# Longer score bursts from step 32, wider feed-forward groups and a re-ranked instruction order in a fused attention and feed-forward kernel

## The chip, the core and the metric

The kernel runs on one core of one Trainium2 chip. That core has a matrix engine (TensorE, PE in the profile; its weight loads are the row PEld), a vector engine (VectorE, DVE), a scalar engine (ScalarE, ACT), a general engine (GpSimd, POOL), an engine that issues transfers (SyncE, SP), and 16 DMA engines. Matmuls write to PSUM, all other tiles lie in SBUF.

The metric is the device time of one execution in microseconds. The kernel before took 552.31 us in the median of 3 runs (551.3 to 552.72). The profiled execution took 550.8 us, and its span from the first to the last instruction was 549.0 us.

## The reference

Thresholded attention over 64 heads (8 batches of 8) of 576 rows and width 64, and after it a gated feed-forward layer over the 4608 rows that result:

```python
scores = q @ k.T / 8
scores = where(scores >= max(scores) - tau, scores, -1e9)     # per row, tau 0.02
attn   = exp(scores - max(scores)) / (sum + 1e-9)
x      = (attn @ v), heads side by side                       # 4608 x 512
xn     = x / sqrt(mean(x * x) + 1e-6) * rms_g
out    = (silu(xn @ w_gate) * (xn @ w_val)) @ w_out           # 512 -> 1536 -> 512
```

Inputs and the output are float32. Scores are computed from float32 operands; the products with `v` and all of the feed-forward layer use float16 operands.

## The kernel before

A **step** is 128 rows of scores for one pair of heads; there are 144 of them. Four steps make a **chunk**: 128 complete rows of `x`. There are 36 chunks. One step goes through these stages:

- S: TensorE writes the scores of both heads into PSUM (`s_ps[0]`, `s_ps[1]`, two banks of 512 columns each, one buffer).
- TTR: VectorE copies them to SBUF with the sign turned and keeps the row's extreme value.
- GpSimd makes the threshold; ScalarE and GpSimd make the masked exponentials (`wsb`).
- `wsb` is transposed, by TensorE with a VectorE copy in the first 16 steps and by a DMA afterwards (`wt`).
- AV: after every second step, TensorE multiplies by `v`; VectorE divides by the row sums (`half`).
- After a whole chunk: square, mean, norm, and a DMA that transposes it to `xnT`.

The feed-forward layer takes **groups** of 2 or 4 chunks. For each of the 12 slices `fc` of 128 hidden columns, four gate matmuls and four value matmuls fill one PSUM buffer each (`ring`, four buffers, and the four banks of `s_ps` when the last scores have been read); ScalarE makes a tanh, VectorE makes the silu and the gated product `hf`. Output matmuls follow, with an evacuation `osb` and a store.

Each such piece of work is an `Op` with an engine, a guessed cost, a priority and its dependencies. A list scheduler fixes the order of each engine's instructions when the program is built; nothing is reordered on the chip by it.

```python
                k = (t + (BIAS if other else 0.0), o.prio, i)   # earliest start first, then priority
                if cand is None or k < cand:
                    cand = k
```

Scores go in bursts. One step has its own burst up to step `SB`; from there a burst fills 1024 columns, which is 1.78 steps:

```python
    def plan_bursts():
        plan = [([(s, 0, S, ROW_AT)], s, [[(s, 0, S // 2, ROW_AT), (s, S // 2, S, 512)]])
                for s in range(min(SB, len(steps)))]
        end = S * (len(steps) - SB)
        for at in range(0, end, 1024):
            ...                                  # segments of one or more steps, split at the bank
            plan.append((segs, SB + at / S, [r for r in runs if r]))
```

```python
    # S: every burst waits for the TTRs of the burst before
    deps = [x for d, _, _ in info.values() for x in d] + last_ttr
    ...
    nc.tensor.matmul(s_ps[h][rows, at:at + hi - lo], lhs(hs), kT[i][p][h][hs, lo:hi], start=True, stop=True)   # L581
    ...
    # TTR: one per head and segment, a step that is cut between two bursts has two per head
    nc.vector.tensor_tensor_reduce(                                                                           # L614
        out=ssb_of(s)[:, h, lo:hi], in0=s_ps[h][:, at:at + hi - lo], in1=zrow[:, lo:hi], scale=-1.0 / 8.0, ...
        accum_out=(mx if last else mxp)[m][:, h:h + 1])
    t = ttr_of[s, h] = add("DVE", ..., s - 1 + TTR_PRIO, made + [o_c] + held + before, ttr)
```

```python
    # feed-forward, n = 128 * chunks of the group
            def gmm(o, fs=fs):
                for d in range(4):
                    nc.tensor.matmul(ring[o.slot[0]][:, 0:n], wg[d][:, fs], xnT[slot][:, d, 0:n], ...)        # L854, vmm is L859
            def tanh(...):  nc.scalar.activation(out=th[i][:, 0:n], ...)                                      # L868
            def silu(...):  nc.vector.scalar_tensor_tensor(out=sl[i][:, 0:n], ...)                            # L871
            def gate(...):  nc.vector.tensor_tensor(out=hf[hi][:, 0:n], ...)                                  # L876
    # output: L924 (L899 in the last group), its evacuation on ScalarE (L939) or VectorE (L937)
            on_dve = streamed and not late or not streamed and OUT_DVE[ci % len(OUT_DVE)]
```

Other lines of the profile: L306 transposes q and k on TensorE and L319 (VectorE) and L317 (ScalarE) copy them to `qkt`; L715 and L724 transpose `wsb` on TensorE and copy it in the first 16 steps; L748 and L753 are AV; L770 and L771 are `half`; L788 to L800 are the norm of a chunk.

Of the kernel before, what the change touches and what calls it, by code (L numbers as in the profile page):

```python
# [13 lines left out]
LAT = dict(PE=200.0, ACT=130.0, DVE=175.0, POOL=20.0, SP=0.0)  # L14
SELF = dict(PE=0.0, ACT=125.0, DVE=178.0, POOL=0.0, SP=0.0)
COST = dict(
    s_main=965.0, s_virt=960.0, tr_qk=530.0, tr4=230.0, tr_full=440.0, av_main=290.0, av_virt=370.0, ffn4=215.0, warm=3500.0,
    evac_qk=600.0, evac_qk_act=465.0, evac_half=252.0, evac_kt=330.0, evac_kt_act=252.0, prelu=667.0, exp2=1060.0, exp1=666.0, exp0=590.0,
    mask_d=680.0, mask_g=1810.0, take_g=1360.0, trw=510.0, evac_w=400.0, evac_wp=900.0, rz=210.0, xmul=341.0, sq=612.0, xn=773.0,
    pool_tiny=302.0, pool_mean=944.0, pool_dma=880.0, cast_v=620.0, cast_vt=475.0, cast_w=665.0,  # L20
# [1 line left out]
)  # L22
DMA_NS = dict(qk=1250.0, tl=700.0, v=880.0, vt=350.0, wt=1700.0, xt=800.0, out=800.0, w=820.0, wo=2500.0)
SWITCH = 125.0


class Op:
# [16 lines left out]
def order_ops(ops, ring_sizes):  # L44


    import heapq

    ring_free = {r: [(0.0, i) for i in range(n)] for r, n in ring_sizes.items()}
    users = {}  # L50
    left = {}
    for i, o in enumerate(ops):
        left[i] = len(o.deps)
        for d in o.deps:
            users.setdefault(id(d), []).append(i)
    pending = {}
    for i, o in enumerate(ops):
        pending.setdefault(o.eng, [])
        if not left[i]:
            pending[o.eng].append(i)  # L60
    eng_free = {e: 700.0 for e in pending}
    dma_free = 0.0
    mode = 0
    out = []
    ready_at = {i: 0.0 for i in range(len(ops))}
    while len(out) < len(ops):
        best = None
        for e, lst in pending.items():
            if not lst:
                continue  # L70
            t0 = eng_free[e]
            cand = None
            for i in lst:
                o = ops[i]
                t = max(t0, ready_at[i])
                if o.ring is not None:
                    free = [f for f in ring_free[o.ring] if o.pick is None or f[1] in o.pick]
                    if len(free) < o.nring:
                        continue
                    t = max(t, sorted(free)[o.nring - 1][0])  # L80
                other = e == "PE" and o.mode != mode
                t = max(t, o.release)
                if o.bulk:
                    t = max(t, dma_free - BACKLOG)
                k = (t + (BIAS if other else 0.0), o.prio, i)
                if cand is None or k < cand:
                    cand = k
            if cand is not None and (best is None or cand < best[0]):
                best = (cand, e)
        (t, _, i), e = best  # L90
        o = ops[i]
        cost = o.cost
        if e == "PE":
            if o.mode != mode:
                t -= BIAS
                cost += SWITCH
            mode = o.mode
        o.start = t
        if o.ring is not None:
            o.slot = []  # L100
            for _ in range(o.nring):
                got = min(f for f in ring_free[o.ring] if o.pick is None or f[1] in o.pick)
                ring_free[o.ring].remove(got)
                o.slot.append(got[1])
        eng_free[e] = t + cost
        if o.dma:
            dma_free = max(dma_free, t + 300.0) + o.dma
            o.end = max(dma_free, t + o.cost) + (LAT_TR if o.cost == COST["sp_tr"] else LAT_LD if o.bulk else 2000.0)
        else:
            o.end = t + cost  # L110
        if o.frees is not None:
            ring_free["R"].append((o.end + LAT[o.eng], o.frees[0].slot[o.frees[1]]))
        for slot in o.opens:
            ring_free["R"].append((o.end + LAT[o.eng], slot))
        pending[e].remove(i)
        out.append(o)
        for j in users.get(id(o), []):
            u = ops[j]
            wait = 60.0 if o.dma else SELF[o.eng] if u.eng == o.eng else LAT[o.eng]
            ready_at[j] = max(ready_at[j], o.end + wait)  # L120
            left[j] -= 1
            if not left[j]:
                pending[u.eng].append(j)
    return out
# [3 lines left out]
def kernel(  # L128
# [12 lines left out]
    nc = tc.nc  # L141
    B, H, S, D = q.shape
    NT, DM = out.shape
# [61 lines left out]
    hf = [sb(f"hf{i}", [128, 512], FP16) for i in range(12)]  # L205
    hf += [stg.bitcast(FP16)[:, 512 * i:512 * (i + 1)] for i in range(NHF - 12)]
    osb = [sb(f"osb{i}", [128, DM]) for i in range(2)]

    s_ps = [ps(f"s_ps{h}", 1024) for h in range(2)]
    ROW_AT = 512 - S // 2  # L210
# [356 lines left out]
    def emit_burst(segs, prio, runs):  # L567
# [5 lines left out]
        for run in runs:  # L573
            def fn(o, run=run):
                for s, lo, hi, at in run:
                    _, whole, quads = info[s]
                    p = steps[s][1]
                    for rows, i, lhs in quads if no_whole or o.quad else whole:
                        for h in range(2):
                            hs = HALF[h]  # L580
                            nc.tensor.matmul(s_ps[h][rows, at:at + hi - lo], lhs(hs), kT[i][p][h][hs, lo:hi],  # L581
                                             start=True, stop=True)

            n = sum(hi - lo for _, lo, hi, _ in run)
            o = add("PE", COST["s_main"] * n / S if not no_whole else COST["s_virt"] * n / S, prio if not made else -600.0,
                    deps + made[-1:], fn, mode=2 if no_whole else 1)
            if not made and REL_N[0] <= prio < REL_N[1]:
                o.release = REL[0] + REL[1] * prio
            made.append(o)
# [13 lines left out]
        for s, lo, hi, at in segs:  # L603
# [7 lines left out]
            for h in range(2):  # L611
                def ttr(o, s=s, lo=lo, hi=hi, at=at, h=h, first=first, last=last):
                    m = s % 6
                    nc.vector.tensor_tensor_reduce(  # L614
                        out=ssb_of(s)[:, h, lo:hi], in0=s_ps[h][:, at:at + hi - lo], in1=zrow[:, lo:hi],
                        scale=-1.0 / 8.0, scalar=3.0e38 if first else mxp[m][:, h:h + 1], op0=ALU.add, op1=ALU.min,
                        accum_out=(mx if last else mxp)[m][:, h:h + 1])

                before = [] if first else [ttr_of[s, h]]
                t = ttr_of[s, h] = add("DVE", 75.0 + (hi - lo) / 0.96, s - 1 + TTR_PRIO, made + [o_c] + held + before, ttr)  # L620
                last_ttr.append(t)

    last_ttr = []
# [1 line left out]
    ssb_user = {}  # L625

    def plan_bursts():
        plan = [([(s, 0, S, ROW_AT)], s, [[(s, 0, S // 2, ROW_AT), (s, S // 2, S, 512)]]) for s in range(min(SB, len(steps)))]
        end = S * (len(steps) - SB)
        for at in range(0, end, 1024):  # L630
            segs, runs = [], [[], []]
            stop = min(end, at + 1024)
            x = at
            while x < stop:
                s, lo = divmod(x, S)
                n = min(S - lo, stop - x)
                segs.append((SB + s, lo, lo + n, x - at))
                x += n
            for s, lo, hi, col in segs:
                for bank in range(2):  # L640
                    a, b = max(col, 512 * bank), min(col + hi - lo, 512 * bank + 512)
                    if a < b:
                        runs[bank].append((s, lo + a - col, lo + b - col, a))
            plan.append((segs, SB + at / S, [r for r in runs if r]))
        return plan

    def emit_softmax(s):
# [183 lines left out]
    def emit_ffn(slot, parts, ready_step, pace, streamed):  # L831
# [6 lines left out]
        clock[0] = st + pace * n / 512.0  # L838
        xops = [t for _, t in parts]
        hs = []  # L840
        mm = 4 * (COST["ffn4"] if n == 512 else 112.0 if n == 256 else 60.0)
        el = n / 0.96 + 65.0
        uses = []
        for fc in range(NFC):
# [42 lines left out]
        if streamed:  # L887

            acc = None

            turns = [(fc, tuple(range(len(parts)))) for fc in range(NFC - BY_ROW)]
            turns += [(fc, (j,)) for j in range(len(parts)) for fc in range(NFC - BY_ROW, NFC)]
            last_out = {}
            for n_, (fc, js) in enumerate(turns):
                hi, m_ = hs[fc]

                def omm(o, fc=fc, hi=hi, js=js, first=acc):
                    for j in js:
                        nc.tensor.matmul(ring[(first or o).slot[j]], hf[hi][:, 128 * j:128 * (j + 1)], wo[:, fc],  # L899
                                         start=(fc == 0), stop=(fc == NFC - 1))  # L900

                late = len(js) == 1 and js[0]
# [9 lines left out]
        for j, (ci, _) in enumerate(parts):  # L912
            kind, b, c = chunks[ci]
            pr = st + dt * (NFC + (j + OUT_AT) * (NFC / len(parts) if SPREAD and not streamed else 1.0))
            oi = count["o"] % 2
            count["o"] += 1
            if streamed:
                mo, at = acc, j
            else:
                mo, at = None, 0  # L920
                for lo in range(0, NFC, OUT_PART):
# [124 lines left out]
            o.fn(o)  # L1046


PACE = 13.0
SQ_DVE = (0,)  # L1050
OUT_DVE = (0,)
LAGS = ()
SB = 64
TTR_PRIO = 1.0
BY_ROW = 4
ACC = (4, 6)
OPENS = ((4,), (6,))
NHF = 24
SPREAD = True
OUT_AT = 0.0  # L1060
PART_PRIO = 1.0
SIZES = (2, 2, 2, 2, 4, 4, 4, 4, 4, 4, 2, 2)
LAG = 16.0
LAT_TR = 3000.0
LAT_LD = 2000.0
REL = (0.0, 0.0)
# [64 lines left out]
```

## Time and profile before

| engine | busy us | share of the span |
|---|---|---|
| PE | 540.8 | 98% |
| VectorE | 434.0 | 79% |
| ScalarE | 450.8 | 82% |
| GpSimd | 323.3 | 59% |

How to read the profile that follows in the prediction:

- "Busy" of TensorE counts each matmul from its start to its modelled end, and matmuls overlap. What a group of matmuls takes from the engine's time is read in the timeline, as the distance from its start to the start of the next group.
- A timeline line holds the start in us, the duration in us of the merged lines, the engine, the source line, the operation, what it writes and reads, the shape, and how many instructions it merges. A piece in square brackets is idle time before it and what ended it.
- The chain of waits starts at the last instruction and goes back to what released each one.
- In the list of waits the columns are who waited, for whom, the total in us, how often, and the longest one.

The same stages in five stretches of the execution, as busy us of each engine:

| stretch, us | PE | VectorE | ScalarE | GpSimd |
|---|---|---|---|---|
| 10 to 30 | 18.54 | 16.15 | 18.96 | 8.11 |
| 30 to 60 | 28.55 | 26.65 | 26.59 | 24.29 |
| 60 to 210 | 149.88 | 122.80 | 134.51 | 102.83 |
| 210 to 477 | 266.66 | 225.31 | 238.85 | 180.50 |
| 477 to 549 | 68.35 | 39.07 | 28.24 | 6.65 |

The last scores are computed at 477 us; after that only AV of the last steps and the feed-forward layer remain. Step 64, where the longer bursts begin, lies at about 218 us.

### The profile page before, as it was taken

What the parts mean: (1) busy time and instruction counts of PE and PEld (TensorE: products, weight loads), DVE (VectorE), ACT (ScalarE), POOL (GpSimd) and SP (SyncE); (2) the same over time, 40 slices, a digit from 0 to 9 for tenths busy, and PEclk for the clock granted to TensorE, in tenths of its full rate; (3) what the DMA queues carried; (4) which work ended last, traced back from release to release, by engine and by line L of the source; (5) the groups of instructions that cost most, each with busy time, mean ns of one, the idle gap of its engine ahead of it and who ended that gap; (6) DMA issues with size and microseconds to landing.
All of it is one profiled execution on the core that took longest, in us unless ns stands there. A gap on an engine that the chain in (4) does not pass through costs nothing.

```text
span 549.0 us, 15126 instructions
## 1 busy us (share of the span) xinstructions
PE 540.8 (98%) x5664; PEld 313.9 (57%) x5664; DVE 434.0 (79%) x1251; ACT 450.8 (82%) x741; POOL 323.3 (59%) x462
## 2 busy tenths in 40 slices
PE   8999999999999999999999999999999999999997
PEld 4656766666667555545555556555655454455764
DVE  4898978888778688878896889798897889775633
ACT  5999888999888889788988899899899988853332
POOL 2377955876777567665767466677767665631000
PEclk9999999999999999999999999999999999999999
DMA  9999999869998698798998698999897666740111
GB/s 197 263 297 267 160 186 212 160 127 190 179 200 175 133 169 156 165 196 158 177 204 154 129 193 184 187 168 213 179 178 158 125 124 90 157 95 29 40 59 57
DMA packets 270025, 89.07 MB, mean 162 GB/s; under 512 B 252544, under 2 KB 262272, under 8 KB 269952
## 3 DMA queue, kind: packets, MB, share of 16 engines
q1 hardware_dynamic: 267168, 86.02, 78.8%
q0 software_dynamic: 1600, 1.57, 1.9%
q8 instruction: 44, 0.72, 0.5%
q10 hardware_dynamic: 1184, 0.52, 0.3%
q14 instruction: 29, 0.24, 0.2%
HBM read 37.75 MB, written 9.44 MB: 86 GB/s over the span
## 4 chain that ended last, share of the span: by engine, by line
PE 92%; DVE 3%; ACT 2%; DMA 1%; POOL 1%; issue 1%; SPq 0%; DVEq 0%
PE s_ps L581 28%; PE ring L854 16%; PE ring L859 16%; PE ring L924 15%; PE ring L753 6%; PE ring L306 2%; PE ring L748 2%; DVE ssb L614 2%; PE s_ps L859 1%; PE s_ps L854 1%; DMA stg<-in_moe_w_gate_dram 1%; PE s_ps L899 1%; PE s_ps L924 1%; ACT ssb L663 1%; PE s_ps L264 1%
## 5 line engine op out<-in xcount | busy, mean ns | idle before, releaser
L614 DVE CUSTOM_DVE_ANT_0 ssb<-s_ps,zrow 128x576 f32<-128x576 f32 (+8 forms) x288 | 182.1, 669 | 25.8 <-PE s_ps L581 21.6
L663 ACT ACTIVATE ssb<-ssb,nth 128x576 f32<-128x576 f32 x224 | 166.5, 767 | 21.7 <-POOL nth L652 21.3
L581 PE MATMUL s_ps<-qkt 64*64 64x288 f32 (+16 forms) x1688 | 158.2, 415 | 2.2 <-DVE mx L614 1.8
L696 POOL TENSOR_SCALAR wsb<-ssb,nth 128x576 f16<-128x576 f32 x64 | 110.6, 1729 | 8.9 <-DMA wt<-wsb 2.7
L581 PEld LDWEIGHTS s_ps<-qkt 64*64 64x64 f32 (+1 forms) x1688 | 77.1, 144 | 59.2 <-issue 20.0
L854 PE MATMUL ring<-xnT,wg 128*128 128x256 f16 (+1 forms) x536 | 109.7, 327 | 0.1
L859 PE MATMUL ring<-xnT,wv 128*128 128x256 f16 (+1 forms) x536 | 109.7, 327 | 0.0
L652 POOL TENSOR_SCALAR nth<-mx 128x2 f32<-128x2 f32 x144 | 31.9, 222 | 107.5 <-DVE mx L614 94.5
L670 ACT ACTIVATE wsb<-ssb 128x1152 f16<-128x1152 f32 x80 | 92.8, 1160 | 1.5 <-DMA wt<-wsb 0.4
L871 DVE SCALAR_TENSOR_TENSOR sl<-th,ring 128x512 f32<-128x512 f32 (+1 forms) x134 | 73.6, 551 | 24.4 <-ACT th L868 23.7
L701 POOL TENSOR_TENSOR wsb<-wsb,esb 128x576 f16<-128x576 f16 x64 | 82.0, 1281 | 9.4 <-ACT esb L682 4.9
L868 ACT ACTIVATE th<-ring 128x512 f32<-128x512 f32 (+1 forms) x134 | 64.4, 482 | 21.5 <-PE ring L854 18.2
L859 PEld LDWEIGHTS <-wv 128*128 128x128 f16 x576 | 52.9, 98 | 41.9 <-issue 8.7
L854 PEld LDWEIGHTS <-wg 128*128 128x128 f16 x576 | 53.2, 98 | 39.9 <-issue 6.6
L614 DVE CUSTOM_DVE_ANT_0 ssb<-s_ps,zrow,mxp 128x128 f32<-128x128 f32 (+7 forms) x80 | 38.2, 515 | 24.4 <-PE s_ps L581 24.0
L682 ACT ACTIVATE esb<-ssb,nth 128x576 f16<-128x576 f32 x64 | 49.2, 769 | 7.2 <-POOL nth L652 7.0
L753 PE MATMUL ring<-va,wt 128*128 128x65 f16 (+1 forms) x1280 | 50.9, 193 | 0.0
L924 PE MATMUL ring<-wo,hf 128*128 128x512 f16 x204 | 48.4, 379 | 0.0
L753 PEld LDWEIGHTS <-wt 128*128 128x128 f16 (+1 forms) x1280 | 46.1, 100 | 3.0
L667 ACT ACTIVATE wsb<-ssb 128x576 f16<-128x576 f32 x64 | 43.6, 681 | 1.1
L924 PE MATMUL ring<-wo,stg 128*128 128x512 f16 x180 | 42.2, 379 | 0.0
L876 DVE TENSOR_TENSOR hf<-ring,sl 128x512 f16<-128x512 f32 (+1 forms) x68 | 38.3, 563 | 4.0
(71 smaller groups left out, 566.7 us busy)
## 6 DMA issues: line engine op xcount, KB each, us to landing
vst<-in_v_dram SPq DMA_DIRECT2D x32, 256.0 KB, 3.6
qkn<-in_k_dram SPq DMA_DIRECT2D x31, 256.0 KB, 4.5
out_dram<-osb SPq DMA_DIRECT2D x31, 256.0 KB, 2.7
qkn<-in_q_dram SPq DMA_DIRECT2D x28, 256.0 KB, 4.5
stg<-in_moe_w_gate_dram SPq DMA_DIRECT2D x6, 512.0 KB, 6.3
stg<-in_moe_w_val_dram SPq DMA_DIRECT2D x6, 512.0 KB, 6.1
wt<-wsb SPq DMA_TRANSPOSE x128, 3.4
wo<-in_moe_w_out_dram POOLq DMA_DIRECT2D x4, 384.0 KB, 6.7
```

The lines of the kernel that those rows point to most:

```text
L581: nc.tensor.matmul(s_ps[h][rows, at:at + hi - lo], lhs(hs), kT[i][p][h][hs, lo:hi], start=True, stop=True)
L614: nc.vector.tensor_tensor_reduce(out=ssb_of(s)[:, h, lo:hi], in0=s_ps[h][:, at:at + hi - lo], in1=zrow[:, lo:hi], scale=-1.0 / 8.0, scalar ...
L663: nc.scalar.activation(out=sb_[:, h], in_=sb_[:, h], func=PRELU, scale=-1.0, bias=nth[m][:, h:h + 1], **PRELU_KW)
L670: nc.scalar.activation(out=wsb[s % NW], in_=sb_, func=AF.Exp)
L696: nc.gpsimd.tensor_scalar(out=wsb[s % NW][:, h], in0=sb_[:, h], scalar1=nth[m][:, h:h + 1], scalar2=None, op0=ALU.is_le)
L701: nc.gpsimd.tensor_tensor(out=wsb[s % NW][:, h], in0=wsb[s % NW][:, h], in1=esb[es], op=ALU.mult)
L753: nc.tensor.matmul(ring[o.slot[0]][rs, at:at + D + 1], w[:, 5 * h + j, rs], va[vi][:, p, 2 * j + h], start=False, stop=(h == 1 and j == 3))
L854: nc.tensor.matmul(ring[o.slot[0]][:, 0:n], wg[d][:, fs], xnT[slot][:, d, 0:n], start=(d == 0), stop=(d == 3))
L859: nc.tensor.matmul(ring[o.slot[0]][:, 0:n], wv[d][:, fs], xnT[slot][:, d, 0:n], start=(d == 0), stop=(d == 3))
L868: nc.scalar.activation(out=th[i][:, 0:n], in_=ring[g.slot[0]][:, 0:n], func=AF.Tanh, scale=0.5)
L871: nc.vector.scalar_tensor_tensor(out=sl[i][:, 0:n], in0=th[i][:, 0:n], scalar=1.0, in1=ring[g.slot[0]][:, 0:n], op0=ALU.add, op1=ALU.mult)
L924: nc.tensor.matmul(ring[(first or o).slot[0]], hf[hs[fc][0]][:, 128 * j:128 * (j + 1)], wo[:, fc], start=(fc == 0), stop=(fc == NFC - 1))
```

## The change

Five things change; the arithmetic stays what it was.

1. Bursts of 1024 columns begin at step 32 and no longer at step 64.
2. The feed-forward groups are 2, 2 and eight times 4 chunks; before they were 2, 2, 2, 2, six times 4, 2, 2. The last group, whose output matmuls are interleaved with its gate and value matmuls, so has 4 chunks and uses all four banks of `s_ps` as accumulators. Its third and fourth result use free score buffers as staging.
3. The evacuations of the output go to VectorE and no longer to ScalarE (`OUT_DVE`).
4. Feed-forward work is paced at 16 steps per 4 chunks (before 13) and released 8 steps after its chunks (before 16).
5. The scheduler adds a fixed offset to the priority of each kind of work (`RANK`), and its guesses of some costs are changed. That moves instructions on every engine's queue. `HOLD` is empty, so the first key of the order is the earliest start, as before.

It is for fewer switches between kinds of matmul on TensorE, for fewer half-width matmuls, and for an order in which TensorE waits less.

```diff
-    s_main=965.0, s_virt=960.0, tr_qk=530.0, tr4=230.0, tr_full=440.0, av_main=290.0, av_virt=370.0, ffn4=215.0, warm=3500.0,
+    s_main=965.0, s_virt=960.0, tr_qk=570.0, tr4=230.0, tr_full=440.0, av_main=300.0, av_virt=370.0, ffn4=215.8, warm=3500.0,
...
+RANK = dict(
+    ACT={"emit_ffn/ev": 110, "emit_ffn/store": -50, "emit_ffn/tanh": -20, ... "emit_qk/ev": -40, "emit_softmax/ex": 10, "emit_softmax/prelu": 60, ...},
+    DVE={"emit_av/half": -120, "emit_burst/ttr": 31, "emit_ffn/ev": 250, "emit_ffn/gate": 90, "emit_ffn/silu": 29, ... "emit_qk/ev": 90, "emit_softmax/ev": 180, ...},
+    PE={"emit_av/fn": 1, "emit_burst/fn": -1.1, "emit_ffn/gmm": 5.1, "emit_ffn/omm": 4.4, "emit_ffn/vmm": 0.7, ...},
+    POOL={...}, SP={...},
+)
...
+    for o in ops:
+        if o.prio > -90.0:
+            path = o.fn.__qualname__.split(".")
+            o.prio += RANK[o.eng].get(..., 0.0)
...
-                k = (t + (BIAS if other else 0.0), o.prio, i)
-                if cand is None or k < cand:
-                    cand = k
+                t += BIAS if other else 0.0
+                opts.append((t, o.prio, i))
+            if opts:
+                soon = min(opts)[0] + HOLD.get(e, 0.0)
+                cand = min((x for x in opts if x[0] <= soon), key=lambda x: (x[1], x[0], x[2]))
...
+    osb += [ssb[0][:, 0, 0:DM], ssb[0][:, 0, 0:DM], ssb[1][:, 0, 0:DM], ssb[2][:, 0, 0:DM]]
...
     def plan_bursts():
-        plan = [... for s in range(min(SB, len(steps)))]
-        end = S * (len(steps) - SB)
-        for at in range(0, end, 1024):
+        plan, s = [], 0
+        for lo, hi in CHOP:
+            plan += [... for x in range(s, lo)]
+            end = S * (hi - lo)
+            for at in range(0, end, 1024):
...
-PACE = 13.0
+PACE = 16.0
+HOLD = {}
-OUT_DVE = (0,)
+OUT_DVE = (1,)
-SB = 64
-TTR_PRIO = 1.0
+CHOP = ((32, 144),)
+TTR_PRIO = 0.0
-ACC = (4, 6)
-OPENS = ((4,), (6,))
+ACC = (4, 5, 6, 7)
+OPENS = ((4, 5), (6, 7))
-PART_PRIO = 1.0
-SIZES = (2, 2, 2, 2, 4, 4, 4, 4, 4, 4, 2, 2)
-LAG = 16.0
+PART_PRIO = 2.0
+SIZES = (2, 2, 4, 4, 4, 4, 4, 4, 4, 4)
+LAG = 8.0
```

## The prediction

> **What bounds the kernel now.** I read the page's first two parts first, then the chain, then the timeline of TensorE in three places, and last the list of waits.

> ```profile
> PE 540.8 (98%) x5664; PEld 313.9 (57%) x5664; DVE 434.0 (79%) x1251; ACT 450.8 (82%) x741; POOL 323.3 (59%) x462
> ...
> PE   8999999999999999999999999999999999999997
> ...
> PE 92%; DVE 3%; ACT 2%; DMA 1%; POOL 1%; issue 1%; SPq 0%; DVEq 0%
> ```

> The reader should see that TensorE is on the path nearly from end to end: 98% busy, and 92% of the chain that ended last. A busy share says little by itself when matmuls overlap, so I read starts in the timeline. Two places, steps with a burst of their own and bursts of 1024 columns:

> ```profile
> 154.78 0.60 PE L854 MATMUL ring<-xnT,wg 128*128 128x256 f16 x4
> 155.22 0.60 PE L859 MATMUL ring<-xnT,wv 128*128 128x256 f16 x4
> 155.66 0.60 PE L854 MATMUL ring<-xnT,wg 128*128 128x256 f16 x4
> 156.19 1.20 PE L581 MATMUL s_ps<-qkt 64*64 64x288 f32 x16
> 157.32 0.61 PE L859 MATMUL ring<-xnT,wv 128*128 128x256 f16 x4
> ```
> ```profile
> 223.21 1.03 PE L859 MATMUL ring<-xnT,wv 128*128 128x512 f16 x4
> 224.17 1.96 PE L581 MATMUL s_ps<-qkt 64*64 64x128 f32 x32
> 226.06 1.04 PE L854 MATMUL ring<-xnT,wg 128*128 128x512 f16 x4
> 226.93 1.03 PE L859 MATMUL ring<-xnT,wv 128*128 128x512 f16 x4
> ```

> From start to start: four matmuls of 256 columns take 0.44 us, of 512 columns 0.87. A single step's scores take 1.13 and the group ahead of them 0.53 in place of 0.44, so entering a score burst costs another 0.09. A burst of 1024 columns takes 1.89, and the 512-column group ahead of it 0.96 in place of 0.87. The same four numbers recur wherever I look between 65 and 545 us, so nearly all of this time is work of TensorE, not waiting. Waiting stands at the start:

> ```profile
> PEld s_ps L581 <- DVE mx L614: 6.5, 14, 0.9
> ...
> PE s_ps L581 <- DVE mx L614: 1.8, 5, 0.4
> ```

> These lines are the list of waits for 0 to 65 us alone: TensorE waits for VectorE to empty `s_ps`. The chain from 36 to 52 us shows how:

> ```profile
> 47.73 0.66 DVE ssb L614
> 48.39 0.01 DVE mx L614
> 48.40 0.60 DVE qkt L319
> 49.00 0.66 DVE ssb L614
> 49.66 0.02 DVE mx L614
> 49.69 0.04 issue
> 49.73 1.20 PE s_ps L581 x14
> ```

> A copy of `qkt` stands between the two TTRs of one step, and the next scores (49.73) wait for the second TTR. I estimate the waiting of TensorE at some 14 us up to 65 us: 14 steps from the scores at 12.10 to those at 55.28 in the chain are 3.08 us each, while the work in a step (1.13 scores, about 0.5 transposes, 0.3 AV, some qkt transposes) is about 2.2; that is 12, and about 2 in the fill before.

> [...] the group at 226.06 is busy for 1.04 us, but the next begins after 0.87. [...] 0.87 / 4 is 217 ns, 0.44 / 4 is 110. [...] the copy holds the TTR behind it for 0.60 us. [...]

> **The change part by part.** Counts are from the two instruction orders that the programs were built with.

> (a) Bursts. Steps 32 to 63 lose 32 single bursts, 24 in four quarters (64*64) at 1.13 and 8 in two halves (64*128) at 1.08 (207.19 to 208.27 in the timeline): 27.1 + 8.6 = 35.7 us, with entry 32 x 0.09 = 2.9, together 38.6. They gain 18 long bursts, 12 at 1.89 and 6 with half-form parts at 1.83 to 1.89, say 1.85: 22.7 + 11.1 = 33.8, and 18 x 0.09 = 1.6, together 35.4. Difference: -3.2 us, all on TensorE's path.

> (b) Groups. 144 gate and value groups of 256 columns become 48, and 144 of 512 become 192. 96 x 0.44 = 42.2 go, 48 x 0.87 = 41.8 come: -0.4 us. Output matmuls, AV and transposes keep their counts.

> (c) Order in the first 16 steps. In the order before, four steps up to the first silu have a copy or a `half` between their two TTRs; in the order after none has, and one `qkt` copy less stands before the first silu. The copies move to where VectorE waits for scores anyway (0.67 us before the TTR at 42.06). Four times 0.6 is 2.4; some of it returns as another wait, so -2 us.

> (d) Single steps between 143 and 161 us are delayed in the kernel before: the scores at 152.38 take 1.79 in place of 1.13. These are long bursts afterwards: I take -1 us, half of what I see there.

> (e) VectorE gains 32 evacuations at 0.69 us (L937) = 22 us, and TTRs of 32 more steps in cut form. TTR is busy 62.75 us for 44 single steps between 65 and 210, 1.43 each, and 126.11 us for 80 steps after that, 1.58: +5. It loses 48 of the 72 narrow silu and gate pairs (0.84) and gains 24 wide ones (1.37): -7. So 434 + 20 = 454, 83% of the span. ScalarE loses 33 evacuations (0.585) and 4 us of tanh: 451 - 23 = 428. Both stay beside TensorE; no change of the time.

> (f) Tighter spots. From the last AV of a group to its first gate matmul the order leaves 8.2, 9.0 and 9.1 us of TensorE work in three of ten groups (by the slots above); before, the least was 8.8 and all others were over 11. The path in between is seen at the end of the kernel before: AV ends at 493.8, the transposing DMA is issued at 496.91 and lands 2.8 us later, about 6 us with no queue in the way. Two or three us are left for queues on VectorE, ScalarE and SyncE. I charge +1 us in all.

> Sum: -3.2 - 0.4 - 2 - 1 + 1 = -5.6. The gap between span and device time stays. 552.3 - 5.6 = 546.7; with the new order tuned as a whole, I lean a little lower: **546.0 us**.

> **The rivals.** *VectorE becomes the bound.* Between 210 and 477 us it is busy 225.3 of 267 us, 84%; with one evacuation of 0.69 per 14 us it comes to 89%. For: [...] already the one that TensorE waits for. Against: PE showed almost no waits at 84%. If it happened, scores would wait for TTRs through the whole middle: 552 to 556. *The feed-forward layer runs dry* at steps 35 to 43, where the first group of 4 chunks is just complete: the order has only 3.1 to 3.2 us of other matmul work between bursts there. A long burst needs 1.89 for scores and about 2.8 for its TTRs (126.11 us for 45 bursts) before the next, so 2.8 is the least that hides it. It has a margin of 0.3; a run with the same density in the kernel before (steps 112 to 130) shows no stall. If it failed: +2 to +4, 549 to 551. *The tail stalls*: after the last scores TensorE has 62 us of work in place of 69, and the last group of 4 chunks begins 8 us after the last AV in place of 33. If its norm and transpose come late, +2 to +3. *The start gains far more*: if the new order removed most of the 14 us of early waiting, 538 to 541. Against: each step there goes through scores and both TTRs in turn, about 2.8 us, whatever the order.

> **Range and chances.** The work terms (a) and (b) are sure within 1 us. (c) and (d) can lie between -8 and 0, (f) and the rivals between 0 and +6. That gives 541 to 551 for 8 in 10. The limit for faster by over 2% is 541.3, which needs most of the early waiting gone: 0.12. Slower by over 2% is above 563.4 and needs VectorE as the bound: 0.03. Within 2%: 0.85.

> **What would show it.** (a) Long bursts of 1.89 us from step 32 on and no 1.13 after it. (c) The wait of scores for `mx` up to 65 us falls from 8.3 to about 6. (d) No score group over 2.0 us after 100 us. (e) VectorE at about 454 us and TensorE still over 97% busy. (f) Waits of gate matmuls for `xnT` stay under 1 us each. The prediction is wrong if TensorE waits for VectorE in the middle, or if the last group's first gate matmul starts over 9 us after the last AV.

## The result, and the profile after

The changed kernel took 550.33 us in the median of 4 executions (550.01 to 550.43) against 552.42 for the kernel before (4 executions, 551.3 to 552.72): a ratio of 0.9965, 95% interval 0.9948 to 0.9982. Timed once more (a0, 6 executions against 11) it took 549.77 against 552.35 us: 0.9954, interval 0.9936 to 0.9971. So the gain is 2.1 to 2.6 us where 6.3 were forecast; the time lies in the range of the forecast, close to its upper end.

From the page of the changed kernel: busy time, TensorE in 40 slices, and the shares of the chain that ended last.

```profile
PE 535.6 (98%) x5444; PEld 296.4 (54%) x5444; DVE 452.5 (83%) x1300; ACT 432.8 (79%) x684; POOL 322.0 (59%) x462
...
PE   8899999999999999999999999999999999999996
...
PE 78%; DMA 7%; DVE 7%; ACT 2%; POOL 2%; issue 2%; SPq 2%; DVEq 0%; POOLq 0%; ACTq 0%
```

TensorE is still 98% busy, with 5.2 us less of it. But it makes up 78% of the chain and no longer 92%; transfers have 7% (1% before) and VectorE 7% (3%). A chain leaves the busiest engine only where that engine waited. So work went away, and waiting came.

To split the two I gave each group of TensorE in the trace its usual slot (single scores 1.13 or 1.07 us, long bursts 1.82 to 1.94 by form, gate and value 0.437 at 256 and 0.863 at 512 columns, output 0.216 a matmul, each the median distance to the next start after 65 us in the kernel before, 0.09 more ahead of scores, and so on) and counted what a group takes beyond it as waiting. Each line is from the trace of one execution, in us; the stretches are named by the steps of the scores:

| trace | slots (work) | waiting | to step 16 | 16 to 32 | 32 to 64 | 64 to 142 | after the scores |
|---|---|---|---|---|---|---|---|
| before | 524.8 | 19.3 | 13.4 | 1.5 | 2.7 | 1.6 | 0.1 |
| after | 521.0 | 22.0 | 13.0 | 2.3 | 3.9 | 2.1 | 0.7 |
| after, again (a0) | 521.0 | 22.2 | 12.2 | 2.3 | 4.5 | 2.5 | 0.7 |

The work fell by 3.8 us, as steps (a) and (b) have it. The waiting did not fall, it rose by 2.7. (With slots chosen in another way, near the fastest of each form in all traces, the same pair gives -2.9 and +1.8, so such a number is good to about 1 us.) After TensorE's last matmul another 4.19 us pass, 3.67 before. Together -3.8 + 2.7 + 0.5 = -0.6, and the spans of the two profiled executions indeed differ by 0.6 only (549.02 and 548.45 us). The medians differ by more, because the profiled execution of the kernel before (550.8 us) was faster than every other one timed (551.1 us at the least); the last section comes back to that.

**The start.** From the list of waits for 0 to 65 us (who waited, for whom, us in total, times, longest):

```profile
PEld L741 <- ACT wsb L696: 8.9, 12, 1.7
...
PE ring L741 <- ACT wsb L696: 3.9, 7, 1.5
PEld s_ps L604 <- DVE mx L637: 3.2, 11, 0.5
```

The waits of scores for `mx` have fallen from 6.5 and 1.8 to 3.2. In their place the transposes of `wsb` (L741) wait for ScalarE; the list of the kernel before has no such line (there these transposes are L715). The timelines of GpSimd and of TensorE show the longest of these:

```profile
17.82 0.63 POOL L512 TENSOR_SCALAR va<-vst 128x512 f16<-128x512 f32 x1 [2.60 <-DMA vst<-in_v_dram]
18.52 0.51 POOL L678 TENSOR_SCALAR nth<-mx 128x2 f32<-128x2 f32 x2
```
```profile
21.47 0.68 PE L741 MATMUL ring<-id,wsb 128*128 128x128 f16 x9 [1.55 <-ACT wsb L696]
```

The threshold `nth` of a step stands in GpSimd's queue behind a cast of `v` (L512), and the cast waits 2.60 us for its load. ScalarE gets the threshold late, and TensorE idles 1.55 us. In the second trace (a0) that load landed some 2 us earlier and this wait wasn't there: waiting to step 8 was 6.3 us in place of 8.0.

**The middle.** TensorE's timeline of the changed kernel at the steps 37 to 41:

```profile
124.13 1.96 PE L604 MATMUL s_ps<-qkt 64*64 64x384 f32 x32
126.03 1.04 PE L880 MATMUL ring<-xnT,wg 128*128 128x512 f16 x4
126.90 1.03 PE L885 MATMUL ring<-xnT,wv 128*128 128x512 f16 x4
127.76 1.03 PE L880 MATMUL ring<-xnT,wg 128*128 128x512 f16 x4
129.52 0.46 PE L329 MATMUL ring<-id,qkn 64*128 64x64 f32 x8 [0.73 <-DVE mxp L637]
130.28 0.46 PE L329 MATMUL ring<-id,qkn 64*128 64x64 f32 x8 [0.29 <-DMA qkn<-in_q_dram]
130.67 1.95 PE L604 MATMUL s_ps<-qkt 64*64 64x512 f32 x16
```

The long burst at 124.13 takes 1.90 to the next start, and the 512-column group 0.87: the slots of step (a). Then a 512-column group lasts from 127.76 to 129.52, twice its slot, and the transposes of q and k come in two halves. This spot costs 1.4 us, and 0.8 in the second trace (a0). It is the thinnest place of the order, where the first group of 4 chunks is just complete.

### The profile page after: what moved, and what is told of

Read it like the earlier page. It is cut to its first block, busy times and chain, and to the rows that moved or that the text cites. A ratio compares the mean times of both kernels' runs of the same rounds, so it can differ in the third digit from the quotient of the medians.

```text
span 548.5 us, 14654 instructions
## 1 busy us (share of the span) xinstructions
PE 535.6 (98%) x5444; PEld 296.4 (54%) x5444; DVE 452.5 (83%) x1300; ACT 432.8 (79%) x684; POOL 322.0 (59%) x462
## 4 chain that ended last, share of the span: by engine, by line
PE 78%; DMA 7%; DVE 7%; ACT 2%; POOL 2%; issue 2%; SPq 2%; DVEq 0%; POOLq 0%; ACTq 0%
PE s_ps L604 23%; PE ring L880 14%; PE ring L951 14%; PE ring L885 13%; PE ring L779 5%; DVE ssb L637 3%; PE ring L329 2%; DMA qkn<-in_q_dram 2%; PE ring L774 2%; PE s_ps L926 2%; DMA vst<-in_v_dram 2%; DMA stg<-in_moe_w_val_dram 1%; DMA stg<-in_moe_w_gate_dram 1%; PE s_ps L885 1%; DVE sl L897 1%
## 5 line engine op out<-in xcount | busy, mean ns | idle before, releaser
L637 DVE CUSTOM_DVE_ANT_0 ssb<-s_ps,zrow 128x576 f32<-128x576 f32 (+8 forms) x288 | 172.8, 635 | 12.4 <-PE s_ps L604 10.9
L604 PE MATMUL s_ps<-qkt 64*64 64x288 f32 (+17 forms) x1660 | 154.0, 414 | 0.8 <-ACT ssb L689 0.4
L880 PE MATMUL ring<-xnT,wg 128*128 128x512 f16 (+1 forms) x456 | 107.0, 357 | 0.0
L885 PE MATMUL ring<-xnT,wv 128*128 128x512 f16 (+1 forms) x448 | 104.8, 356 | 0.0
L894 ACT ACTIVATE th<-ring 128x512 f32<-128x512 f32 (+1 forms) x114 | 61.4, 540 | 39.2 <-PE ring L880 39.1
L637 DVE CUSTOM_DVE_ANT_0 ssb<-s_ps,zrow,mxp 128x128 f32<-128x128 f32 (+7 forms) x112 | 53.5, 515 | 30.4 <-PE s_ps L604 29.6
L885 PEld LDWEIGHTS <-wv 128*128 128x128 f16 x480 | 45.7, 98 | 47.2 <-issue 3.8
L880 PEld LDWEIGHTS <-wg 128*128 128x128 f16 x480 | 42.6, 98 | 43.4 <-issue 6.8
L951 PE MATMUL ring<-wo,stg 128*128 128x512 f16 x168 | 39.2, 379 | 0.0
L902 DVE TENSOR_TENSOR stg<-ring,sl 128x512 f16<-128x512 f32 (+1 forms) x56 | 35.1, 631 | 3.8 <-DVE sl L897 0.5
```

The costliest lines, as they stand in the source:

```text
L637: nc.vector.tensor_tensor_reduce(out=ssb_of(s)[:, h, lo:hi], in0=s_ps[h][:, at:at + hi - lo], in1=zrow[:, lo:hi], scale=-1.0 / 8.0, scalar ...
L885: nc.tensor.matmul(ring[o.slot[0]][:, 0:n], wv[d][:, fs], xnT[slot][:, d, 0:n], start=(d == 0), stop=(d == 3))
L894: nc.scalar.activation(out=th[i][:, 0:n], in_=ring[g.slot[0]][:, 0:n], func=AF.Tanh, scale=0.5)
L951: nc.tensor.matmul(ring[(first or o).slot[0]], hf[hs[fc][0]][:, 128 * j:128 * (j + 1)], wo[:, fc], start=(fc == 0), stop=(fc == NFC - 1))
```

## The experiments

Each was timed in turns with the kernel before, whose medians were 551.76, 551.79, 552.35 and 552.54 us in the four series. Ratios are against the kernel before. Waiting and slots are counted as above.

### Bursts alone, in both orders

e1, kernel before:

```diff
-SB = 64
+SB = 32
```

> The kernel before with one number changed: long bursts from step 32 in place of step 64; groups, pace, evacuations and priorities as before (the list scheduler makes a new order from it). Theory A, bursts are worth what their slots say and the gain was lost elsewhere: -2 to -4 us against before, with 18 fewer score entries' worth of work on TensorE. Theory B, longer bursts bring their own waits (one score buffer, TTR of 2.8 us per burst): between -1 and +2 us, and waits of scores for mx or mxp between 107 and 215 us grow by 2 us or more.

Measured: 556.28 us, ratio 1.0071 (1.005 to 1.0092). It is slower by 4.5 us though its slots are 3.4 us less (521.4). The waiting grew to 28.6 us; 8.3 of that in steps 32 to 64, where the kernel before has 2.7. (In its profiled execution the start is 2.2 us longer too; the clock was granted at 0.74 in the mean from 30 to 35 us, which by the estimate of the last section is up to 1.7 of it.) The slots shrink as worked out, and more than that comes back as waiting. That is theory B in direction, but the loss is larger than it said and lies elsewhere: the waits of scores for `mx` and `mxp` between 107 and 215 us did not grow (4.3 us, 5.0 before). Some 4 of the added 5.6 us stand in the slots of narrow gate and value groups in this stretch, which lost 0.2 us before.

e7, kernel after with the bursts of before:

```diff
-CHOP = ((32, 144),)
+CHOP = ((64, 144),)
```

> Kernel after with bursts of 1024 columns from step 64 as before (CHOP), all else as after. If the slot arithmetic of step (a) is the whole of it: 3.2 us more, 553.0 to 554.0 us. Rival (the long bursts in steps 32 to 43 brought the wait of 1.9 us at 128 us, so it goes with them): 551.0 to 552.0 us. Third (single steps delay as in the kernel before, step (d)): 554.0 to 555.5 us.

Measured: 556.69 us, 1.008 (1.0061 to 1.0099), slower than all three expectations. Its slots are 524.4, that is +3.4, again as in step (a). Waiting in steps 32 to 64 fell to 2.2 us, as the rival had it. But 4.9 us of waiting stand after the last scores, where the kernel after has 0.7: the longest of them, 1.5 us in the last feed-forward group but one, is for a PSUM buffer that a division of AV frees late (1.33 us before 503.02 us, for `xsb`), and in the last group the output matmuls stop twice, 0.9 us each, for an evacuation on VectorE. So neither kernel's order carries the other's bursts.

### The offsets alone

e2, kernel after:

```diff
-RANK = dict(ACT={"emit_ffn/ev": 110, ...}, ...)
+RANK = dict(ACT={}, DVE={}, PE={}, POOL={}, SP={})
```

> Kernel after with every offset of RANK set to zero; bursts, groups, pacing and the place of the evacuations stay. Theory A (the offsets are what the long bursts need: with the old priorities they bring waits of their own in steps 32 to 64, as the bursts alone did): 553 to 557 us. Rival (wider groups and slower pacing already take those waits away, the offsets are worth under 1 us): 549.5 to 551.5 us.

Measured: 559.32 us, 1.0129 (1.0101 to 1.0156). Theory A, and more than it expected. TensorE's timeline and one stretch of the table by windows (the stretch and its length; busy us of PE, PEld, DVE, ACT and POOL, each with its number of instructions; then the mean granted clock, DMA share, GB/s):

```profile
124.80 3.90 PE L592 MATMUL s_ps<-qkt 64*128 64x256 f32 x16 [2.34 <-DVE mxp L625]
131.10 3.71 PE L592 MATMUL s_ps<-qkt 64*64 64x384 f32 x32 [2.41 <-DVE mxp L625]
```
```profile
125.00:130.00 5.00, 3.70 (x16) 2.83 (x16) 1.64 (x7) 3.13 (x5) 3.34 (x6) 0.67 0.55 112
```

Between two bursts TensorE has nothing but AV: the output of one group is done at 117 us and the next group isn't there yet. It waits 2.4 us for the TTRs of the burst before, and then the clock is granted at 0.67 in the mean of this stretch and bursts take 3.7 to 3.9 us, where the one at 113.96 us took 1.96 with the clock at 1.00. This is the rival "the feed-forward layer runs dry". With all offsets gone the filling work is no longer spread over that place; which of the offsets does it was not tried.

### Bursts and the width of the groups

e10, kernel before with both:

```diff
-SB = 64
-SIZES = (2, 2, 2, 2, 4, 4, 4, 4, 4, 4, 2, 2)
+SB = 32
+SIZES = (2, 2, 4, 4, 4, 4, 4, 4, 4, 2, 2)
```

> Kernel before with bursts of 1024 columns from step 32 and groups of 2, 2, seven times 4, 2, 2 chunks; no offsets, pacing as before. Theory A (long bursts need wide groups: a burst keeps VectorE in TTRs for 2.8 us, four ring buffers hold 4 x 0.44 = 1.8 us of TensorE work at 256 columns and 3.5 us at 512): the waits that the bursts alone brought between 100 and 210 us (TensorE idle 3.7 us there) fall to under 1.5 us, and the time to 551 to 553 us. Rival B (the wide group completes too late, the feed-forward layer runs dry at steps 35 to 43, as without the offsets): TensorE idle over 4 us between 100 and 140 us, 555 to 560 us.

Measured: 554.6 us, 1.0041 (1.0028 to 1.0055), 1.7 us less than the bursts alone. Both theories show: the layer runs dry at 121 us, where two bursts follow each other and take 6.5 us, against some 3.7 for two slots (B), while from step 46 to 64 the waiting is 1.5 us against 3.6 with narrow groups (A).

e11, kernel after, and e16, which adds CHOP = ((64, 144),) to it:

```diff
-SIZES = (2, 2, 4, 4, 4, 4, 4, 4, 4, 4)
+SIZES = (2, 2, 2, 2, 2, 2, 4, 4, 4, 4, 4, 4)
```

> Kernel after with six groups of 2 chunks and then six of 4, all else as after. Theory A (bursts need wide groups): slots of gate and value matmuls of 256 columns lengthen between 100 and 210 us, by 2 to 4 us in all, 552.5 to 555 us. Rival B (only step (b) of the prediction, 0.4 us): 550.3 to 551.5 us. Third (smaller groups come sooner and fill the thin spot at steps 35 to 43): 548.5 to 550 us.

> Kernel after with six groups of 2 chunks and six of 4, and bursts of 1024 columns from step 64 only: the fourth corner in the order of the kernel after. Theory A (the waits of 8.8 us in slots of 256 columns come from long bursts together with narrow groups): those slots lose under 2 us, 553 to 556 us. Rival B (narrow groups wait by themselves with this pacing, whatever the bursts): the slots still lose over 6 us, 561 to 565 us.

Measured: e11 561.55 us (1.0166, 1.0151 to 1.018) and e16 559.87 us (1.0128, 1.0111 to 1.0144). The time of e11 is above every expectation; of what theory A named, the slots of 256 columns, 8.8 us are waiting in e11. How one arises, from the timeline of e11:

```profile
126.00 0.60 PE L885 MATMUL ring<-xnT,wv 128*128 128x256 f16 x4
...
126.93 0.42 DVE L897 SCALAR_TENSOR_TENSOR sl<-th,ring 128x256 f32<-128x256 f32 x1
...
127.40 0.60 PE L880 MATMUL ring<-xnT,wg 128*128 128x256 f16 x4 [0.80 <-DVE sl L897]
```

TensorE needs a free ring buffer for its next gate group; the silu that frees it (126.93) stands on VectorE behind a TTR (L637, 0.76 us from 126.09). From 126.00 to 127.40 are 1.40 us for a slot of 0.44. In e16 the slots of 256 columns lose 3.1 us, above what A expected (under 2) and well below B's 6; 1.15 and 0.57 of it lie at 220 and 233 us, that is after step 64, where its long bursts begin and narrow groups still run.

e13, the fourth corner in the order of before (only SIZES as in e10):

> Kernel before with groups of 2, 2, seven times 4, 2, 2 chunks; single bursts to step 64, all else as before. The fourth corner of bursts and groups in the order of the kernel before. If only the slots count (step (b), here 72 gate and value groups of 256 columns of 144 joined to 36): 0.2 to 0.3 us less, 551.5 to 552.2 us. Theory A (wide groups help only where long bursts are) leaves that as it is, plus what another order costs by itself (about 2 us in the control): 552 to 555 us, waits of TensorE spread over the execution. Rival (the group completes too late, as at 121 us with the long bursts): TensorE idle over 3 us between 100 and 140 us.

(Of the 144 narrow groups 48 are joined here, to 24, and not 72 to 36; the forecast of 0.2 to 0.3 us is not touched by that.)

Measured: 554.82 us, 1.0048 (1.003 to 1.0066). The layer runs dry here too: at 128 us the scores of two steps follow each other and take 3.7 us, where their slots are 2.2. The corners, medians in us, with the waiting in slots of 256 columns in brackets:

| | bursts from 64 | bursts from 32 |
|---|---|---|
| order of before, narrow early groups | 551.8 to 552.5 (0.8) | 556.28 (4.5) |
| order of before, wide | 554.82 (0.6) | 554.6 (0.9) |
| order of after, narrow early groups | 559.87 (3.1) | 561.55 (8.8) |
| order of after, wide | 556.69 (0.8) | 549.8 to 550.3 (0.7) |

With narrow groups long bursts cost time in both orders (+3.8 to +4.5 and +1.7), with wide ones they don't (-0.2 and -6.4 to -6.9). Each corner is another order too, which in the next experiment is worth some 2 us by itself. The waiting in the narrow slots depends less on that (1.3 us in the next experiment, 0.8 in the kernel before), and it is largest where both meet. The brackets count fewer slots where groups are wide (48 or 96 of 256 columns in place of 144). In all gate and value slots between 105 and 220 us (steps 32 to 64), of 256 or 512 columns, the waiting is, row by row, 0.4 and 4.8, 0.1 and 1.5, 1.7 and 6.5, 0.2 and 1.1 to 1.6 us: the same picture. What fits the sizes is the room in the ring: a long burst keeps VectorE about 2.8 us in TTRs (126.11 us for 45 bursts in the kernel before); four ring buffers are 4 x 0.44 = 1.8 us of TensorE's work at 256 columns, and 4 x 0.87 = 3.5 at 512. The number of buffers was not varied, so this reason is argued and not shown.

### An order by itself

e12, kernel before: no work changes, only a priority.

```diff
-TTR_PRIO = 1.0
+TTR_PRIO = 0.0
```

> A control: kernel before with the TTR priority of the kernel after (0 in place of 1), which changes no work and only the order. Theory A (the kernel before sits in a tuned order, and any other costs some us whatever it is for): 553 to 557 us, all of the difference being waits of TensorE. Rival B (an order matters little by itself): 551.3 to 552.3 us.

Measured: 554.42 us, 1.0036 (1.0022 to 1.0049): 2.1 us for nothing but another order, with slots of 524.8 as before and 4.8 us of waiting in steps 64 to 142 in place of 1.6. Theory A for this order; e9 below is another order that costs nothing. So up to some 2 us of any single part above may be the price of leaving a tuned order, and only what exceeds it, or what a count of waits shows, says something of the part. The pacing (`PACE`, `LAG`) and the guesses of costs were not changed by themselves.

### The start: step (c) by itself

e9, kernel before: what stands between the two TTRs of a step is moved behind the second, in the first 16 steps. The work is the same, the values that come out are not, so this run speaks of the time alone.

> The kernel before with four places on VectorE's queue changed: in the four of the first 16 steps where a qkt copy or a half stood between the two TTRs of a step, it comes after the second TTR. All else is as in before. Theory A, the prediction's step on the early order (each costs TensorE 0.6 us): -1.5 to -2.4 us. Theory B, ScalarE, busy 19 of 20 us between 10 and 30, sets the pace there, so scores that come earlier only wait for the exponentials: 0 to -0.6 us, and waits for mx are replaced by waits for wsb.

Measured: 552.14 us, 1.0004 (0.9983 to 1.0024).

e9b does it the other way, with the values left as they are:

```diff
+    for s in range(16):
+        first, second = sorted((of[s, 0], of[s, 1]), key=seq.index)
+        seq.remove(second)
+        seq.insert(seq.index(first) + 1, second)
```

> Kernel before; in the first 16 steps the second TTR of a step is moved directly behind the first one on VectorE, so copies that stood between them come after. Theory A (ScalarE and GpSimd set the pace of the first steps, 2.6 to 2.95 us of ScalarE a step): no gain, 551.5 to 552.5 us; TensorE's waits of scores for mx up to 65 us fall from 8.3 to under 6 us, but waits for copies or for wsb rise by as much. Theory B (step (c) of the prediction: the copy between the TTRs costs 0.6 us in four steps): 549.5 to 550.5 us.

Measured: 554.25 us, 1.0026 (1.0003 to 1.0049). Two executions at full clock took 551.84 and 552.15 us, four with a mean clock of 0.996 or 0.997 took 554.09 to 555.88. Neither e9 nor e9b gains anything: theory B of e9 and theory A of e9b as to the time. Waits of scores for `mx` fell less than it expected (6.4 and 1.0 us), and a wait of 1.6 us of a transpose of `wsb` for a delayed `qkt` copy came instead. The copy between two TTRs is not what sets the pace. That ScalarE does fits the numbers, but nothing here made ScalarE faster by itself.

### Two queue places in the kernel after

e3: the thresholds of steps 2 and 3 ahead of the third and fourth cast of `v` on GpSimd.

```diff
+    for i in (2, 3):
+        move_after(v_cast[i], tn_of[i])
```

> The kernel after with two neighbours on GpSimd's queue exchanged: the threshold of step 2 ahead of the third cast of v, which waits for its transfer until 17.7 us. All else is as in after. Theory A, this one queue place holds ScalarE up by 2.8 us, and ScalarE sets the pace of the first steps: -1.5 to -2.8 us against after (about 548), and TensorE's wait of 1.55 us for wsb at 21 us is gone. Theory B, the first steps go at the pace of scores and TTR: under 0.5 us.

Measured: 548.52 us, 0.9939 (0.9916 to 0.9961). The wait at 20 us is gone, and waiting to step 16 is 12.3 us, against 13.0 in the first trace of the kernel after; but it was 12.2 in the second, where the load came in time by itself. In the trace of e3 it came early as well (the cast starts at 16.34 us, in place of 17.82), so the trace doesn't tell what the exchange is worth.

e4: the pair of q and k loads that was late at 128 us is issued six places earlier on SyncE.

```diff
+    front = on_sp[on_sp.index(pair[0][0]) - 6]
+    for ld, before in pair:
+        seq.remove(ld)
+        seq.insert(seq.index(front), ld)
```

> The kernel after with one pair of transfers, q and k of the first head pair of the fourth batch, 6 places further ahead on SyncE's queue (issued at about 113 in place of 124 us). Theory A, TensorE waits for this pair at 128 to 130 us because it stands behind transposing transfers that wait for their sources: -1 to -1.6 us against after, and no gap at 128 to 130. Theory B, the wait is for VectorE as the profile's line names it (mxp): no change of the time, the gap stays.

Measured: 548.7 us, 0.9935 (0.9913 to 0.9957). TensorE's timeline at the same place:

```profile
127.72 1.03 PE L882 MATMUL ring<-xnT,wg 128*128 128x512 f16 x4
128.68 0.71 PE L331 MATMUL ring<-id,qkn 64*128 64x64 f32 x16
129.42 2.08 PE L606 MATMUL s_ps<-qkt 64*64 64x512 f32 x16
```

The group at 127.72 has its slot again and the 16 transposes run in one piece. Only the load was moved, so the first wait had been the load's too, although the trace put it down to VectorE's `mxp`; in a0 the line names the load (0.6 us in two waits). (In this execution, as in a0, another 1.4 us are lost at 152 us, where a transposing DMA for `wt` lands late.)

e5: both.

> Kernel after with both queue changes: the thresholds of steps 2 and 3 ahead of the third and fourth cast of v on GpSimd, and one pair of q and k loads six places earlier on SyncE. If the two waits are independent (theory A): 1.8 + 1.6 us less than the kernel after, 546.5 to 547.3 us. Rival (TensorE comes to the same later limit, transfers above all, only sooner): 548.0 to 548.7 us, as either alone.

Measured: 549.02 us, 0.9937 (0.9922 to 0.9952). The gains do not add. All three are faster than the kernel before; their intervals overlap with that of the kernel after (0.9936 to 0.9971), so that they beat it by some 1 us is likely and not shown.

### The evacuations

e8, kernel after:

```diff
-OUT_DVE = (1,)
+OUT_DVE = (0,)
```

> Kernel after with the evacuations of the output on ScalarE as before. Step (e) of the prediction (both engines have room, the time doesn't change): 549.5 to 551 us. Rival (VectorE is freed of 22 us and empties scores and rings sooner): 547 to 549 us. Third (ScalarE is the tighter one and another order costs by itself): 551.5 to 555 us.

Measured: 563.97 us, 1.0191 (1.0169 to 1.0214), far above all three expectations. Beyond the slots stand 37.3 us, 10.7 of them in steps 32 to 64, where transposes wait for loads of q (1.40 us before 132.51), and twice the clock falls (to 0.50 from 22 to 24 us, after 1.9 us without work for TensorE, and again at 128 us, to 0.60 in the mean up to 132). How much is the place of the evacuations and how much the other order stays open.

## Why the prediction was right and wrong

**(a) and (b), work: right.** -3.6 was forecast, -3.8 counted (-2.9 with the other choice of slots), and the bursts alone are 3.4 us of slots in e1 and in e7, -3.2 forecast.

**(c), the early order, -2: wrong.** Counted -0.4, and -1.2 in the second trace. A comparison without slots says the same: the scores of the 16th step start 0.8 and 1.7 us earlier, with 0.6 us less work ahead of them (16 transposes of q and k). The sign of (c) came (scores wait for `mx` 3.2 in place of 8.3 us; I had written about 6), its reason did not: e9 and e9b take the copies away from between the TTRs and gain nothing. What I had left out is that in the first steps each scores group is part of a ring through VectorE, GpSimd's threshold, ScalarE and back to the transposes. ScalarE was busy 18.96 of the 20 us from 10 to 30, and I had that in my own table. The wait moved from `mx` to `wsb`.

**(d), steps 143 to 161, -1: wrong, and the costliest step.** The long single slots did go. But I took the long bursts for work only. In steps 32 to 64 TensorE waits 3.9 to 4.5 us where it waited 2.7, so +1.2 to +1.8 stands where I had -1. That it is the bursts is shown from both sides: added to the order of before they bring 5.6 us of waiting to these steps (e1), and without them the order of after has 2.2 there (e7). The bursts at 111 and 141 us take 2.43 and 2.26, against my sign "no score group over 2.0 us". The first of them, in the kernel after:

```profile
110.82 2.49 PE L604 MATMUL s_ps<-qkt 64*64 64x128 f32 x32
111.36 1.39 PEld L604 LDWEIGHTS s_ps<-qkt 64*64 64x64 f32 x30 [0.35 <-DVE mxp L637]
```

After its first two weight loads the burst waits for the second TTR of the burst before (`mxp`). The two instructions of a `half`, from 109.59 us, stand ahead of that TTR on VectorE.

**The rival "runs dry at steps 35 to 43"** named that place rightly and I gave it too little weight: the kernel after loses 1.4 us at 128 us (0.8 in a0), and in four other orders with wide groups it breaks open (e2, e8, e10, e13; not in e7). I had compared matmul work of 3.1 us with a need of 2.8; transposes of late loads belong to that work and were not there in time (e4). That the whole lies in this rival's 549 to 551 us is in part luck, since most of the difference stands in other places.

**(e), engines: right in numbers,** VectorE 452.5 (454) and ScalarE 432.8 (428), and VectorE did not become the bound. That the place of the evacuations is neutral is not shown: moved back, with the order that results, the time rises by some 14 us (e8).

**(f), tighter spots, +1: too small.** Counted are 0.8 in steps 16 to 32, 0.5 in steps 64 to 142, 0.6 after the scores and 0.5 after TensorE's end, together 2.4. It isn't where I had put it: no gate matmul waits for `xnT` in the list of waits, and the last group's first gate matmul starts 8.0 us after the last AV, within the 9 that I had allowed.

Sum of the counted terms: -3.8 - 0.4 + 1.2 + 2.4 = -0.6, the difference of the two profiled executions. The 1.5 to 2.0 us by which the medians differ more are in no term. The further lean from 546.7 to 546.0, for an order "tuned as a whole", had no measured ground.

## What to carry to other kernels

Price the work of a change by slots, and beside it ask which queue gets longer: compare an uninterrupted run on one engine with what the buffers that this engine frees hold of the other's work (here 2.8 us of TTRs against 1.8 or 3.5). Parts that were tuned together are not judged one by one: take the corners, and a control that changes the order alone. When a wait goes from an engine's list, look for the one that came in its place before booking a gain.

## What was not expected of the hardware

```profile
27.00:28.00 1.00, 0.46 (x6) 0.32 (x5) 0.97 (x4) 1.00 (x3) 0.00 (x0) 1.00 0.98 354
28.00:29.00 1.00, 0.00 (x0) 0.00 (x0) 1.00 (x3) 1.00 (x2) 0.22 (x1) 1.00 1.02 367
...
30.00:31.00 1.00, 1.00 (x19) 0.88 (x19) 0.24 (x2) 0.57 (x3) 0.43 (x2) 0.50 1.15 344
```
```profile
28.46 0.38 PE L715 MATMUL ring<-id,wsb 128*128 128x128 f16 x4 [0.96 <-DVE qkt L319]
...
29.95 2.20 PE L581 MATMUL s_ps<-qkt 64*64 64x288 f32 x16
```

In e9b TensorE is idle from 27.51 to 29.15 us, and the clock is granted at 0.50 from 29.76 to 33.18 us (worked out from the means of the windows: 0.88 from 29 to 30 us, 0.50 in each window up to 33, 0.91 from 33 to 34). Four other traces have low means too: e1 0.74 and e9 0.73 from 30 to 35 us, e2 0.67 from 125 to 130 and from 130 to 135 us, e8 0.50 from 22 to 24 and 0.60 from 128 to 132 us. In e1 the fall lies from 29.18 to 32.59 us (0.59 from 29 to 30 us, 0.70 from 32 to 33), and the scores at 29.95 take 2.20 us, where a single step's take 1.20 in the kernel before. From that I estimate the cost of such a fall at up to half of its 3.41 us, 1.7 us.

In the 3.4 us before the fall TensorE was without a matmul for 1.9 us in e8 (at 22 us), 1.7 in e9b and 1.3 in e1. This time alone does not decide: 1.55 us in the kernel after (up to 21.47 us) and 2.62 us in e10 (up to 125.67 us) were followed by no fall, the clock being granted at 1.00 in the mean from 20 to 32 us and from 100 to 140 us. What else counts stays open.

Executions of the kernel before lie between 551.1 and 554.3 us. Six of 44 had a mean clock of 0.996 or 0.997, where one such fall would put it (half of 3.41 us in 550 is 0.003), and they took 552.28 us or more; none of the ten of the kernel after (548.3 to 551.4 us) was below 0.998. So a part of the measured gain beyond the 0.6 us between the two profiled executions may be this fall being avoided. It is not all: ten executions of the kernel before took 553 us and more at 0.999 or 1.0, and what delays those stays open, since no trace of one was taken.
